# Weights' low words cut to three bits on ScalarE in place, and a cosine as one sine with a quarter turn

## The chip, the cores and the metric

The kernel runs on one core of a Trainium2 chip. Times are microseconds (us) of device time for one execution. TensorE is PE (PEld its weight loads), VectorE is DVE, ScalarE is ACT, GpSimd is POOL; SP is the engine whose queue issues all DMAs here.

## The reference

```python
def _attn_ref(q, k, v):                 # q, k, v: float32 (4, 8, 768, 64)
    for t in range(S):
        state = gamma * state + einsum('bhd,bhe->bhde', k[:, :, t], v[:, :, t])
        y[:, :, t] = scale * einsum('bhd,bhde->bhe', q[:, :, t], state)

def _moe_ref(x, w_in, w_out):           # x (3072, 512), w_in (512, 2048), w_out (2048, 512)
    h = x @ w_in
    g = h * np.cos(h)
    return g @ w_out

def _moe2_ref(x, w_in, w_out):
    h = x @ w_in
    g = np.where(h > 0.0, h, np.exp(np.minimum(h, 0.0)) - 1.0)
    return g @ w_out
```

The result is retention attention, then the first layer pair with `h * cos(h)`, then the second with ELU. The four weight matrices come as float64.

## The kernel before, in words

All code is in `retention_then_two_mlps`. It runs in five stages: the attention by units of 128 tokens (24 units, 4 batches each); the first hidden layer, by 6 blocks of 512 tokens times 8 tiles j of 256 hidden features (`hidden`); the first projection (`project(0, ...)`), by 3 superblocks of two blocks; the second hidden layer (`hidden2`, 24 steps through `seven`); the second projection (`project(1, ...)`). From the first projection on, the products are made with seven block products instead of eight, so operands are summed and subtracted beforehand. Every matmul operand is split in a high and a low part (fp32r), and three matmuls of 512 columns make one product: ACT writes the high part, DVE then subtracts it to get the low one.

Weights: `to_f32` (line 349) brings the float64 words to float32 in 32 pieces of 1024 columns, each in two halves of 512. A half is loaded as pairs of 32-bit words into a buffer `raw` (tag "c"). ACT multiplies the upper words, read as float32, by `REBIAS` into `t`; ACT then writes the same values as float16 into the upper two bytes of each word of the tile `signs`, of which the sign bit is wanted. On DVE, line 374 shifts `t` left by 3 and ors `signs` in, and line 377 ors in the raw low word shifted right by 29, its upper three bits. `first_weights` uses this for the first layer's `w_in` (8 pieces, during the opening and the first block), `convert` for the other three matrices (16 pieces during blocks 1 to 4, 8 during `hidden2`), which are kept in DRAM and split later by `prepare`.

Cosine: `hidden` makes a PSUM tile h of 128x1024. Line 698: ACT writes h / 2 pi rounded to int32 into u. Line 699: DVE takes h / 2 pi - u. Then ACT makes sin(pi x), ACT squares it times 2, and line 704, DVE, makes (g - 1) * h, which is -h cos h; the sign is taken out again by `turn` in `prepare` for layer 0.

What sets the order: the loops only record operations in `Plan` (engine, planned price, buffers read and written, a lag). `Plan.run` then plays the recording through with a list scheduler: each operation has a due time worked backwards from PE's fixed order, each engine takes the ready one that is due first, and the program is written out in that order, engine by engine. Operations marked "ANY" (sums, subtractions, scalings) go to DVE or POOL, whichever is free first in the planner's clock. So another price, one operation less or another engine changes the order of much else. Each engine executes its own list in order. Buffers come from pools: 11 of tag "c" (4 KB per partition), 8 "w", 4 "hl", 3 "ld", 4 "h", and in PSUM 3 "eg" and 2 "f". A PSUM tile h is free for PE when line 704 has read it.

ACT operations all show as line 332 and tensor_tensor operations as line 337, the helpers `act` and `tt`.

Of the kernel before, what the change touches and what calls it, by code (L numbers as in the profile page):

```python
# [9 lines left out]
F32 = mybir.dt.float32  # L10
F32R = mybir.dt.float32r
BF16 = mybir.dt.bfloat16
F16 = mybir.dt.float16
I32 = mybir.dt.int32
U32 = mybir.dt.uint32
U64 = mybir.dt.uint64
AF = mybir.ActivationFunctionType
ALU = mybir.AluOpType

P = 128  # L20
# [14 lines left out]
TWO_PI = 2.0 * math.pi  # L35

REBIAS = 2.0**-112

# [259 lines left out]
def retention_then_two_mlps(ctx: ExitStack, tc: tile.TileContext, attn, tab, weights, out):  # L300
    nc = tc.nc
# [10 lines left out]
    plan = Plan(slots)  # L312
# [18 lines left out]
    def act(us, out_, in_, r, w, func=AF.Copy, lag=0, **kw):  # L331
        plan.op("ACT", us, lambda: nc.scalar.activation(out=out_(), in_=in_(), func=func, **kw), r, w, lag)  # L332
# [6 lines left out]
        plan.op(eng, us, go, r, w, lag)  # L339


    signs = keep.tile([P, 512], U32, name="signs")
    signs_b = Buf(None, [P, 512], U32)
    signs_b.t = signs
    plan.op("DVE", 0.3, lambda: nc.vector.memset(signs, 0.0), [], [signs_b])

    def to_f32(layer, io, j, lag):  # L350
        t = Buf("c", [P, WS])
        if not wide:
            dma(4, lambda: t.t, lambda: weights[layer, io, j], w=[t], lag=lag)
            return t
        for hh in range(2):
            lo, hi = hh * 512, hh * 512 + 512
            raw = Buf("c", [P, 512, 2], U32)
            dma(
                4, lambda raw=raw: raw.t.rearrange("p n w -> p (n w)"),
                lambda lo=lo, hi=hi: weights[layer, io, j][:, lo:hi].bitcast(U32), w=[raw], lag=lag,  # L360
            )
            act(
                0.65, lambda lo=lo, hi=hi: t.t[:, lo:hi], lambda raw=raw: raw.t[:, :, 1].bitcast(F32),
                [raw], [t[lo, hi]], scale=REBIAS, lag=lag,
            )

            act(
                0.65, lambda: signs.bitcast(F16).rearrange("p (n w) -> p n w", w=2)[:, :, 1],
                lambda lo=lo, hi=hi: t.t[:, lo:hi], [t[lo, hi]], [signs_b], lag=lag,
            )  # L370

            def steps(lo=lo, hi=hi, raw=raw):
                u = lambda: t.t[:, lo:hi].bitcast(U32)
                plan.op("DVE", 0.69, lambda: nc.vector.scalar_tensor_tensor(  # L374
                    out=u(), in0=u(), scalar=3, in1=signs, op0=ALU.logical_shift_left, op1=ALU.bitwise_or,
                ), [t[lo, hi], signs_b], [t[lo, hi]], lag)
                plan.op("DVE", 0.69, lambda: nc.vector.scalar_tensor_tensor(  # L377
                    out=u(), in0=raw.t[:, :, 0], scalar=29, in1=u(),
                    op0=ALU.logical_shift_right, op1=ALU.bitwise_or,
                ), [raw, t[lo, hi]], [t[lo, hi]], lag)  # L380

            steps()
        return t
# [34 lines left out]
    def prepare(layer, io, j, lag=0):  # L418
        k = kept[layer, io][j]
        w = Buf("w", [P, NP, 2, Q], F32R)  # L420
        w_t[layer, io, j] = w
        t, s = Buf("c", [P, WS]), Buf("c", [P, WS])
        dma(4, lambda: t.t, lambda: k.t, [k], [t], lag)

        turn = -1.0 if layer == 0 else 1.0

        def split(src, at, lo, hi):
            view = lambda: src.t[:, 0:(hi - lo) * Q].rearrange("p (n q) -> p n q", q=Q)
            high = lambda: w.t[:, lo:hi, 0, :]
            act(0.1 + 0.26 * (hi - lo), high, view, [at], [w[lo, hi]], lag=lag, scale=turn)  # L430
            plan.op("DVE", 0.08 + 0.29 * (hi - lo), lambda: nc.vector.scalar_tensor_tensor(  # L431
                out=w.t[:, lo:hi, 1, :], in0=view(), scalar=turn, in1=high().bitcast(F32),
                op0=ALU.mult, op1=ALU.subtract,
            ), [at, w[lo, hi]], [w[lo, hi]], lag)

        split(t, t[0, 3 * Q], 0, 3)
        a11, a12, a22, a21 = ((t, q * Q, q * Q + Q) for q in range(4))
        s1, s2, s3, s4 = ((s, q * Q, q * Q + Q) for q in range(4))
        for o, a, b, op in (
            (s1, a21, a22, ALU.add), (s2, s1, a11, ALU.subtract),  # L440
            (s3, a11, a21, ALU.subtract), (s4, a12, s2, ALU.subtract),
        ):
            view = lambda x: (lambda: x[0].t[:, x[1]:x[2]])
            tt("ANY", (0.35, 0.7), view(o), view(a), view(b), op, [a, b], [o], lag=lag)
        split(s, s, 3, NP)
# [221 lines left out]
    def hidden(blk, j, between=()):  # L667
        sb, odd = divmod(blk, 2)
        xh, xl = x_t[blk]
        h = Buf("eg", [P, 2 * TB])  # L670
        for half in range(2):
            fi = half if odd else 1 - half

            def go(half=half, fi=fi):
                n = 0
                for kc in range(KC):
                    qd = ((0, 1), (3, 2))[fi][kc // 2]
                    for wpart, xpart in PARTS:
                        nc.tensor.matmul(  # L679
                            out=h.t[:, half * TB:(half + 1) * TB], lhsT=quarter(j, qd, wpart, kc % 2),  # L680
                            rhs=(xh, xl)[xpart].t[:, kc, :], start=(n == 0), stop=(n == 3 * KC - 1),
                        )
                        n += 1

            need = []
            for qd in ((0, 1), (3, 2))[fi]:
                n = 4 * j + qd
                need.append(win1[n // NP][n % NP])
            plan.op("PE", 12 * MM, go, [xh, xl] + need, [h[half * TB, half * TB + TB]])
            if half == 0:  # L690
                for step, n in between:
                    step(n)
        u = Buf("c", [P, 2 * TB])
        g = Buf("c", [P, 2 * TB])


        n = lambda: u.t.bitcast(I32)
        act(1.0, n, lambda: h.t, [h], [u], scale=1.0 / TWO_PI)
        plan.op("DVE", 1.22, lambda: nc.vector.scalar_tensor_tensor(  # L699
            out=g.t, in0=h.t, scalar=1.0 / TWO_PI, in1=n(), op0=ALU.mult, op1=ALU.subtract,  # L700
        ), [h, u], [g])
        act(1.0, lambda: g.t, lambda: g.t, [g], [g], func=AF.Sin, scale=math.pi)
        act(1.0, lambda: g.t, lambda: g.t, [g], [g], func=AF.Square, scale=math.sqrt(2.0))
        plan.op("DVE", 1.22, lambda: nc.vector.scalar_tensor_tensor(  # L704
            out=g.t, in0=g.t, scalar=1.0, in1=h.t, op0=ALU.subtract, op1=ALU.mult,
        ), [h, g], [g])
        if not odd:
            put(0, sb, j, 2, 4, lambda: g.t, [g], 0)
        elif sb == NSB - 1:
            put(0, sb, j, 0, 2, lambda: g.t, [g], 0)  # L710
        else:
            pair_up(0, sb, j, g, u, 30)
# [463 lines left out]
```

## Time and profile before

| | before |
|---|---|
| runs | 1060.12, 1060.22, 1061.75 us; median 1060.22 |
| profiled execution | 1058.54 us |
| its span, first to last instruction | 1056.8 us |
| PE busy | 1028.8 us (97%), mean granted clock 0.995 |
| DVE busy | 806.6 us (76%) |
| ACT busy | 651.5 us (62%) |
| POOL busy | 230.8 us (22%) |

Durations and waits in the following come from the profiled execution. In a table by stretches, an engine's busy time is that of the stretch and the number behind it how many instructions started or ran in it; instructions on one engine can overlap a little, so a sum of durations is somewhat more than the busy time. PEclk is the TensorE clock granted, 1.00 being full speed (2.4 GHz).

### The profile page before, as it was taken

To read this page: it belongs to the slowest core of one execution; us is meant where nothing else is said; L and a number is where in the kernel's file an instruction comes from. 1 tells how busy PE (TensorE), PEld (TensorE's weight loads), DVE (VectorE), ACT (ScalarE), POOL (GpSimd) and SP (SyncE) were. 2 spreads that over 40 slices of the span, in tenths; PEclk is the share of its full clock that TensorE was granted. 3 is DMA by queue.
4 is the path that set the end of the run, shared out by engine and by line. 5 is a ranking of instruction groups with operands and counts; after the bars stand their busy time and mean duration, and the time that the engine had idled before them with its cause. 6 is when DMAs were issued, how large, how long until landed. Compare 5 with 4: busy or idle time off the path is not lost. (4 is left out here: it accounts for less than half of the span.)

```text
span 1056.8 us, 18290 instructions
## 1 busy us (share of the span) xinstructions
PE 1028.8 (97%) x7204; PEld 832.6 (79%) x7208; DVE 806.6 (76%) x931; ACT 651.5 (62%) x788; POOL 230.8 (22%) x213
## 2 busy tenths in 40 slices
PE   6999999999999999999999999999999999999998
PEld 4667788888888888888888777877778888888886
DVE  5898888888889968657468997878889966466453
ACT  2686567766799753443445877877879743544442
POOL 1222340144224610000001542233334201000000
PEclk9899999999999999999999999999999999999999
DMA  9778799999999999999995668789869999999861
GB/s 347 263 259 302 245 361 314 333 355 356 347 331 352 332 345 347 318 326 383 316 359 195 226 245 304 284 311 338 298 239 299 357 333 351 343 320 323 309 209 70
DMA packets 110101, 323.40 MB, mean 306 GB/s; under 512 B 8640, under 2 KB 8640, under 8 KB 107456
## 3 DMA queue, kind: packets, MB, share of 16 engines
q1 hardware_dynamic: 110016, 322.25, 85.4%
q8 instruction: 56, 0.92, 0.4%
q14 instruction: 29, 0.24, 0.1%
HBM read 195.86 MB, written 126.35 MB: 305 GB/s over the span
## 5 line engine op out<-in xcount | busy, mean ns | idle before, releaser
L925 PE MATMUL eg<-hl,w 128*128 128x512 f32 x2016 | 457.9, 389 | 1.0 <-DVE h L877 0.9
L925 PEld LDWEIGHTS eg<-hl,w 128*128 128x128 f32 x2016 | 378.3, 188 | 80.3 <-DVE h L877 1.4
L332 ACT ACTIVATE hl<-ld 128x1024 fp32r<-128x1024 f32 x168 | 177.7, 1060 | 226.3 <-PE eg L925 206.3
L337 DVE TENSOR_TENSOR hl<-ld,hl 128x1024 fp32r<-128x1024 f32 x168 | 211.6, 1269 | 94.4 <-ACT hl L332 94.3
L679 PE MATMUL eg<-hl,w 128*128 128x512 f32 x1152 | 277.0, 397 | 3.0 <-DVE c L704 1.5
L337 POOL TENSOR_TENSOR c<-c 128x512 f32<-128x512 f32 (+1 forms) x141 | 173.3, 1240 | 479.5 <-DVE c L337 170.4
L332 ACT ACTIVATE c<-c 128x1024 f32<-128x1024 f32 (+1 forms) x256 | 232.1, 918 | 57.7 <-DVE c L699 27.9
L679 PEld LDWEIGHTS eg<-hl,w 128*128 128x128 f32 x1152 | 214.2, 189 | 51.5 <-DVE w L337 1.9
L337 DVE TENSOR_TENSOR c<-c 128x512 f32<-128x512 f32 (+2 forms) x127 | 92.8, 741 | 40.5 <-DMA c<-d 30.0
L332 ACT ACTIVATE c<-eg 128x1024 int32<-128x1024 f32 (+2 forms) x95 | 86.3, 909 | 50.7 <-PE eg L679 43.2
L755 PE MATMUL eg<-hl,w 128*128 128x512 f32 x432 | 110.6, 392 | 2.8 <-DVE c L337 1.4
L755 PEld LDWEIGHTS eg<-hl,w 128*128 128x128 f32 x432 | 80.2, 188 | 23.4 <-DVE c L337 3.0
L755 PE MATMUL eg<-ld,w 128*128 128x512 f32 x288 | 74.1, 393 | 4.6 <-ACT h L332 3.9
L699 DVE SCALAR_TENSOR_TENSOR c<-eg,c 128x1024 f32<-128x1024 f32 x48 | 58.6, 1220 | 19.2 <-ACT c L332 17.1
L755 PEld LDWEIGHTS eg<-ld,w 128*128 128x128 f32 x288 | 53.4, 188 | 18.4 <-ACT h L332 6.0
L704 DVE SCALAR_TENSOR_TENSOR c<-c,eg 128x1024 f32<-128x1024 f32 x48 | 58.3, 1215 | 12.1 <-ACT c L332 11.7
L332 ACT ACTIVATE w<-c 128x1024 fp32r<-128x1024 f32 (+3 forms) x59 | 52.7, 920 | 10.0 <-DMA c<-d 3.6
L431 DVE SCALAR_TENSOR_TENSOR w<-c,w 128x768 fp32r<-128x768 f32 (+1 forms) x48 | 56.2, 1183 | 0.9 <-ACT w L332 0.9
L332 ACT ACTIVATE signs<-c 128x512 f16<-128x512 f32 x64 | 50.2, 785 | 6.5 <-DVE c L374 5.8
L377 DVE SCALAR_TENSOR_TENSOR c<-c 128x512 uint32<-128x512 uint32 x64 | 52.6, 831 | 0.7
L374 DVE SCALAR_TENSOR_TENSOR c<-c,signs 128x512 uint32<-128x512 uint32 x64 | 50.2, 785 | 0.8 <-ACT signs L332 0.5
L332 ACT ACTIVATE h<-eg 128x512 f32<-128x512 f32 (+1 forms) x50 | 29.2, 584 | 29.1 <-PE eg L755 10.7
(58 smaller groups left out, 641.8 us busy)
## 6 DMA issues: line engine op xcount, KB each, us to landing
d<-c SPq DMA_DIRECT2D x205, 512.0 KB, 5.1
ld<-d SPq DMA_DIRECT2D x84, 1024.0 KB, 8.1
c<-d SPq DMA_DIRECT2D x93, 512.0 KB, 6.1
c<-in_weights SPq DMA_DIRECT2D x64, 512.0 KB, 6.6
ld<-in_attn SPq DMA_DIRECT2D x20, 1024.0 KB, 7.8
d<-h SPq DMA_DIRECT2D x32, 256.0 KB, 8.3
out<-c SPq DMA_DIRECT2D x11, 512.0 KB, 7.2
d<-c SPq DMA_DIRECT2D x16, 256.0 KB, 3.8
```

The source lines that it names most:

```text
L332: plan.op("ACT", us, lambda: nc.scalar.activation(out=out_(), in_=in_(), func=func, **kw), r, w, lag)
L337: return e.tensor_tensor(out=out_(), in0=a(), in1=b(), op=op)
L374: plan.op("DVE", 0.69, lambda: nc.vector.scalar_tensor_tensor(out=u(), in0=u(), scalar=3, in1=signs, op0=ALU.logical_shift_left, op1=ALU.b ...
L377: plan.op("DVE", 0.69, lambda: nc.vector.scalar_tensor_tensor(out=u(), in0=raw.t[:, :, 0], scalar=29, in1=u(), op0=ALU.logical_shift_right ...
L431: plan.op("DVE", 0.08 + 0.29 * (hi - lo), lambda: nc.vector.scalar_tensor_tensor(out=w.t[:, lo:hi, 1, :], in0=view(), scalar=turn, in1=hig ...
L679: nc.tensor.matmul(out=h.t[:, half * TB:(half + 1) * TB], lhsT=quarter(j, qd, wpart, kc % 2), rhs=(xh, xl)[xpart].t[:, kc, :], start=(n == ...
L699: plan.op("DVE", 1.22, lambda: nc.vector.scalar_tensor_tensor(out=g.t, in0=h.t, scalar=1.0 / TWO_PI, in1=n(), op0=ALU.mult, op1=ALU.subtra ...
L704: plan.op("DVE", 1.22, lambda: nc.vector.scalar_tensor_tensor(out=g.t, in0=g.t, scalar=1.0, in1=h.t, op0=ALU.subtract, op1=ALU.mult,), [h, ...
L755: nc.tensor.matmul(out=out_(), lhsT=w.t[:, i, wpart, kc * P:(kc + 1) * P], rhs=x.t[:, xpart, kc, :], start=(start and n == 0), stop=(n == ...
L925: nc.tensor.matmul(out=acc.t[:, i * TB:(i + 1) * TB], lhsT=w[:, A_OF[p], wpart, i * P:(i + 1) * P], rhs=hl.t[:, gpart, k, :], start=(p in ...
```

## The change

Weights: the tile `signs` and its memset are gone. ACT multiplies the raw low word, read as an unsigned integer, by 0.936 x 2^-29 and writes it rounded as int16 into the lower two bytes of that same word; ACT writes the float16 of `t` into the upper two bytes. Each low word of `raw` then holds the three bits and the sign, and one DVE step (line 378 now) shifts `t` and ors it in. The second DVE step is gone.

Cosine: the rounding adds 0.25, so the remainder x lies a quarter turn lower; one Sin with scale 2 pi and a bias of pi / 2, read from a [128, 1] tile set once, makes cos h; the Square is gone, and DVE multiplies by h with a plain tensor_tensor. `turn` is 1 for both layers. The planner's price for the Sin is 1.1 where it was 1.0.

```diff
+LOW_BITS = 0.936 * 2.0**-29
...
-    signs = keep.tile([P, 512], U32, name="signs")
-    signs_b = Buf(None, [P, 512], U32)
-    signs_b.t = signs
-    plan.op("DVE", 0.3, lambda: nc.vector.memset(signs, 0.0), [], [signs_b])
+    turn_b = Buf(None, [P, 1])
+    turn_b.t = keep.tile([P, 1], F32, name="quarter_turn")
+    plan.op("DVE", 0.1, lambda: nc.vector.memset(turn_b.t, math.pi / 2), [], [turn_b])
...
+            end = lambda part, dt, raw=raw: raw.t.rearrange("p n w -> p (n w)").bitcast(dt).rearrange(
+                "p (n w) -> p n w", w=4)[:, :, part]
...
-            act(
-                0.65, lambda: signs.bitcast(F16).rearrange("p (n w) -> p n w", w=2)[:, :, 1],
-                lambda lo=lo, hi=hi: t.t[:, lo:hi], [t[lo, hi]], [signs_b], lag=lag,
-            )
+            act(0.65, lambda end=end: end(0, I16), lambda raw=raw: raw.t[:, :, 0], [raw], [raw],
+                scale=LOW_BITS, lag=lag)
+            act(0.65, lambda end=end: end(1, F16), lambda lo=lo, hi=hi: t.t[:, lo:hi],
+                [t[lo, hi]], [raw], lag=lag)
...
                 plan.op("DVE", 0.69, lambda: nc.vector.scalar_tensor_tensor(
-                    out=u(), in0=u(), scalar=3, in1=signs, op0=ALU.logical_shift_left, op1=ALU.bitwise_or,
-                ), [t[lo, hi], signs_b], [t[lo, hi]], lag)
-                plan.op("DVE", 0.69, lambda: nc.vector.scalar_tensor_tensor(
-                    out=u(), in0=raw.t[:, :, 0], scalar=29, in1=u(),
-                    op0=ALU.logical_shift_right, op1=ALU.bitwise_or,
-                ), [raw, t[lo, hi]], [t[lo, hi]], lag)
+                    out=u(), in0=u(), scalar=3, in1=raw.t[:, :, 0], op0=ALU.logical_shift_left, op1=ALU.bitwise_or,
+                ), [t[lo, hi], raw], [t[lo, hi]], lag)
...
-        turn = -1.0 if layer == 0 else 1.0
+        turn = 1.0
...
-        act(1.0, n, lambda: h.t, [h], [u], scale=1.0 / TWO_PI)
+        act(1.0, n, lambda: h.t, [h], [u], scale=1.0 / TWO_PI, bias=0.25)
...
-        act(1.0, lambda: g.t, lambda: g.t, [g], [g], func=AF.Sin, scale=math.pi)
-        act(1.0, lambda: g.t, lambda: g.t, [g], [g], func=AF.Square, scale=math.sqrt(2.0))
-        plan.op("DVE", 1.22, lambda: nc.vector.scalar_tensor_tensor(
-            out=g.t, in0=g.t, scalar=1.0, in1=h.t, op0=ALU.subtract, op1=ALU.mult,
-        ), [h, g], [g])
+        act(1.1, lambda: g.t, lambda: g.t, [g, turn_b], [g], func=AF.Sin, scale=TWO_PI, bias=turn_b.t)
+        tt("DVE", 1.22, lambda: g.t, lambda: g.t, lambda: h.t, ALU.mult, [g, h], [g])
```

PE's order of work stays; the order on the other engines changes in many places. Three of them follow. A name's number tells one buffer from another within a program; they differ between the programs. ACT's helper is line 334 in the changed kernel, `tt` line 339.

DVE in the opening, from the third unit's mask to the end of the attention output (hl) of the first block. Before:

```order
L374 SCALAR_TENSOR_TENSOR c_327<-c_327,signs_81 128x512
L572 COPY w_136<-eg_286 128x256
L377 SCALAR_TENSOR_TENSOR c_327<-c_201,c_327 128x512
L377 SCALAR_TENSOR_TENSOR c_327<-c_206,c_327 128x512
L563 TENSOR_TENSOR w_441<-eg_390,w_136 128x768
L572 COPY w_136<-eg_390 128x256
L374 SCALAR_TENSOR_TENSOR c_387<-c_387,signs_81 128x512
L337 TENSOR_TENSOR hl_339<-f_445,hl_331 128x2x128
L337 TENSOR_TENSOR hl_339<-f_446,hl_331 128x2x128
L337 TENSOR_TENSOR ld_382<-ld_382,w_136 128x512
L337 TENSOR_TENSOR w_443<-c_327,w_443 128x4x256
L337 TENSOR_TENSOR hl_339<-f_481,hl_331 128x2x128
```

And now:

```order
L378 SCALAR_TENSOR_TENSOR c_327<-c_327,c_201 128x512
L378 SCALAR_TENSOR_TENSOR c_327<-c_327,c_206 128x512
L563 TENSOR_TENSOR w_442<-eg_393,w_136 128x768
L339 TENSOR_TENSOR w_434<-c_327,w_434 128x4x256
L572 COPY w_136<-eg_393 128x256
L339 TENSOR_TENSOR hl_339<-f_445,hl_331 128x2x128
L339 TENSOR_TENSOR hl_339<-f_446,hl_331 128x2x128
L339 TENSOR_TENSOR ld_384<-ld_384,w_136 128x512
L378 SCALAR_TENSOR_TENSOR c_389<-c_389,c_341 128x512
L339 TENSOR_TENSOR hl_339<-f_483,hl_331 128x2x128
```

The two shifts of line 377 are gone, and the wide weight split (w_434) has moved ahead of the third unit's pieces.

ACT in the first block, between the int32 conversions (eg) of tiles 1 and 2. Before:

```order
L332 ACTIVATE c_727<-eg_624 128x1024
L332 ACTIVATE c_748<-c_599 128x512
L332 ACTIVATE w_750<-c_597 128x2x256
L332 ACTIVATE signs_81<-c_748 128x512
...
L332 ACTIVATE c_748<-c_637 128x512
L332 ACTIVATE c_798<-eg_730 128x1024
```

The line left out is the pair Sin and Square. And now, where c_595, c_599 and c_639 are raw buffers:

```order
L334 ACTIVATE c_742<-eg_621 128x1024
L334 ACTIVATE w_747<-c_665 128x2x256
L334 ACTIVATE c_595<-c_665 128x512
L334 ACTIVATE c_754<-c_599 128x512
L334 ACTIVATE c_599<-c_599 128x512
L334 ACTIVATE c_751<-c_751,quarter_turn_81 128x1024
L334 ACTIVATE c_754<-c_639 128x512
L334 ACTIVATE c_639<-c_639 128x512
L334 ACTIVATE c_814<-eg_729 128x1024
```

Three two-byte writes stand where there was one, and one wide activation where there were two.

ACT at the entry of the second hidden layer, around the copy of the last projection's tile (c_5845, now c_5793). Before:

```order
L332 ACTIVATE ld_5841<-c_5802 128x1024
L332 ACTIVATE c_5845<-eg_5310 128x1024
L332 ACTIVATE w_5807<-c_5810 128x4x256
L332 ACTIVATE w_5804<-c_5827 128x4x256
L332 ACTIVATE h_5863<-eg_5834 128x512
```

And now:

```order
L334 ACTIVATE c_5793<-eg_5261 128x1024
L334 ACTIVATE ld_5798<-c_5758 128x1024
L334 ACTIVATE ld_5802<-c_5775 128x1024
L334 ACTIVATE w_5756<-c_5778 128x4x256
L334 ACTIVATE h_5810<-eg_5786 128x512
```

Two of the layer's first x2 operands (ld) have moved behind the copy, and the first snapshot (h) comes one activation later.

## Rows read from the trace of the kernel before

**Rows 1.** The page, part 1: busy time, share of the span, instructions.

```profile
PE 1028.8 (97%) x7204; PEld 832.6 (79%) x7208; DVE 806.6 (76%) x931; ACT 651.5 (62%) x788; POOL 230.8 (22%) x213
```

**Rows 2.** Stretches: us, then PE, PEld, DVE, ACT, POOL busy, clock, DMA, GB/s.

```profile
0.00:40.00 40.00, 28.52 (x620) 18.93 (x624) 26.32 (x44) 14.76 (x27) 7.57 (x10) 0.87 0.91 336
40.40:94.20 53.80, 51.00 (x716) 39.65 (x720) 50.77 (x66) 43.57 (x59) 13.88 (x18) 1.00 0.73 258
94.20:375.00 280.80, 280.33 (x2951) 227.62 (x2952) 245.03 (x306) 200.61 (x245) 98.41 (x97) 1.00 0.93 331
...
560.00:790.00 230.00, 221.92 (x959) 178.32 (x958) 197.28 (x238) 177.96 (x239) 77.64 (x59) 1.00 0.75 274
```

**Rows 3.** PE's waits from 0 to 40 us: us in total, times, longest.

```profile
PE f L629 <- issue: 4.8, 2, 3.5
...
PE f L629 <- DVE hl L337: 1.4, 1, 1.4
```

**Rows 4.** PE's waits from 40 to 145 us.

```profile
PE eg L679 <- DVE c L704: 1.5, 3, 0.7
PE eg L536 <- DVE w L578: 0.9, 1, 0.9
PE eg L679 <- DVE w L337: 0.6, 2, 0.3
```

**Rows 5.** PE's waits from 560 to 830 us.

```profile
PE eg L755 <- ACT h L332: 4.8, 6, 1.5
PE eg L755 <- DVE c L337: 2.1, 4, 0.7
PE f L755 <- DVE hl L337: 0.6, 1, 0.6
```

**Rows 6.** Groups by form: shapes and count, then busy us, mean ns, idle before.

```profile
L332 ACT ACTIVATE signs<-c 128x512 f16<-128x512 f32 x64 | 50.2, 785 | 6.5 <-DVE c L374 5.8
L332 ACT ACTIVATE c<-c 128x512 f32<-128x512 f32 x88 | 57.1, 651 | 21.5 <-DMA c<-in_weights 16.6 <-issue 2.3 <-DVE c L337 1.8
L332 ACT ACTIVATE c<-c 128x1024 f32<-128x1024 f32 x168 | 177.6, 1058 | 36.2 <-DVE c L699 27.9 <-DVE c L857 1.4 <-POOL c L337 1.3
L377 DVE SCALAR_TENSOR_TENSOR c<-c 128x512 uint32<-128x512 uint32 x64 | 52.6, 831 | 0.7
L704 DVE SCALAR_TENSOR_TENSOR c<-c,eg 128x1024 f32<-128x1024 f32 x48 | 58.3, 1215 | 12.1 <-ACT c L332 11.7
L337 DVE TENSOR_TENSOR c<-eg,c 128x1024 f32<-128x1024 f32 x18 | 22.0, 1222 | 6.4 <-PE eg L925 4.9 <-DMA d<-c 1.5
```

**Rows 7.** The second stretch, line 377 alone: DVE busy, clock, DMA, GB/s.

```profile
40.40:94.20 53.80, 11.26 (x13) 1.00 0.73 258
```

**Rows 8.** Timeline in the opening, ACT and then DVE: start, us, what.

```profile
22.70 0.78 ACT L332 ACTIVATE signs<-c 128x512 f16<-128x512 f32 x1
23.33 0.67 ACT L332 ACTIVATE c<-c 128x512 f32<-128x512 f32 x1
...
25.77 1.06 ACT L332 ACTIVATE w<-c 128x1024 fp32r<-128x1024 f32 x1 [0.18 <-DVE c L377]
26.73 0.64 ACT L332 ACTIVATE hl<-f 128x256 fp32r<-128x256 f32 x2
...
24.45 1.28 DVE L377 SCALAR_TENSOR_TENSOR c<-c 128x512 uint32<-128x512 uint32 x2
```

**Rows 9.** Timeline of PE, first hidden matmuls: start, us, what, idle before.

```profile
32.10 1.22 PE L679 MATMUL eg<-hl,w 128*128 128x512 f32 x2 [0.33 <-DVE hl L337]
```

**Rows 10.** Stretches of 8 us in the opening (columns as in rows 2).

```profile
24.00:32.00 8.00, 4.72 (x162) 3.54 (x161) 8.00 (x13) 4.92 (x9) 2.96 (x2) 0.89 0.93 329
32.00:40.00 8.00, 7.42 (x23) 5.45 (x23) 6.33 (x12) 4.08 (x7) 1.04 (x1) 0.69 0.82 314
```

**Rows 11.** Timeline of PE at the entry of the second hidden layer.

```profile
586.19 1.65 PE L755 MATMUL eg<-ld,w 128*128 128x512 f32 x6 [0.73 <-ACT h L332]
...
592.87 1.32 PE L755 MATMUL eg<-ld,w 128*128 128x512 f32 x5
```

More of the change, by code (lines that the diff above doesn't have):

```diff
@@ L14 @@
 I32 = mybir.dt.int32
+I16 = mybir.dt.int16
 U32 = mybir.dt.uint32
```

## The prediction

> **What bounds the kernel now.** I read first which engine is busy. TensorE (PE) works through 97% of the span [rows 1]. So no gain can come from an engine's busy time alone: it has to come out of the 28 us in which PE stands still, or out of the time in which it runs at half clock. The table by stretches [rows 2] says where these are: 11.5 us of idle PE in the first 40 us, 2.8 us between 40.4 and 94.2, 0.5 us up to 375, 8.1 us between 560 and 790 (the second hidden layer); the 5 us that are left lie in the projections and at the end, which the change does not touch. In the same table VectorE (DVE) is busy 50.77 of 53.80 us in the second stretch, and 86% of the fourth; ScalarE (ACT) has 81% and 77% there. Then I asked what ended PE's waits. In the opening the largest are PE's own "issue" gaps, 4.8 us, and 1.4 us is for a DVE split of the attention's output [rows 3]. From 40 to 145 us its waits end with a DVE instruction: 1.5 + 0.9 + 0.6 = 3.0 us [rows 4]. In the second layer 4.8 us end with ACT's copies out of PSUM, 2.1 + 0.6 us with DVE [rows 5]. So the stretch in which the change works hardest, the conversion of the first weights, is one in which DVE holds PE up and ACT still has some room.
>
> **The weights: off DVE, onto ACT.** There are 64 halves to convert. Each loses one DVE shift-and-or, 0.831 us in the mean and 52.6 us in all [rows 6]; the remaining one now reads its second operand at the removed one's stride, so it costs that row's 0.831 us at most, in stages where DVE then has room: nothing for PE. Each half gains one ACT instruction, the low word to three bits. The trace has none that reads an integer low word and writes two bytes in every eight. Nearest is the copy that writes the sign half, two bytes in every four: 0.785 us. Below, a 512-wide copy of four-byte values is 0.65 us; above, I allow twice the nearest, 1.57 us. I take 0.785 us for both two-byte writes, since they differ from that row only in stride.
>
> **The cosine.** 48 Square instructions of 1.058 us go from ACT [rows 6], and from the chain that hands a PSUM tile back: PE, ACT to int32, DVE, Sin, Square, DVE. That chain gets about 1.05 us shorter per tile. The last DVE step becomes a plain multiply; the same shape is in the trace at 1.222 us against 1.215, so nothing. The Sin now reads its bias from a tile, which no activation before does; from rows I bound that by nothing at all and by the 0.05 us by which wide activations differ among themselves. The Trainium skill (ScalarE: Activation LUTs, section What ACT_TABLE_LOAD costs) says that a [128,1] pointer operand adds about 93 ns to an activation; no run here shows it yet. By that page 7 Sins would cost ACT 0.65 us in the second stretch, and if all of that reached PE the forecast would be 1057.4 in place of 1056.7.
>
> **Second stretch, 40.4 to 94.2 us.** Between the first and the eighth int32 conversion DVE loses 13 shifts, 11.26 us [rows 7]: 50.77 - 11.26 = 39.5 of 53.8. ACT's order there shows 12 two-byte writes more than the 12 before, 12 four-byte ones where there were 10, and 7 Squares fewer: 43.57 + 12 x 0.785 + 2 x 0.65 - 7 x 1.058 = 46.9 us. PE needs 53.8 less its waits of 2.7 there, 51.1 us. So ACT has 4.2 us to spare and neither engine binds. Following the order tile by tile, the split of the weights for a tile, ACT and then DVE, comes at or before PE's need. I take the 3.0 us of rows 4 as gone.
>
> **Opening.** Before, DVE is busy all the time from 24 to 32 us [rows 10], two shifts (1.28 us) among it [rows 8], and PE gets the last low piece of the attention output at 32.10 us [rows 9]. Now ACT does more first: from 22.70 us two sign halves (23.33 - 22.70 = 0.63 each from start to start), a copy (0.65), a low word (0.63), the wide weight copy (26.73 - 25.77 = 0.96), a copy and a low word, so it copies the third unit's output at 27.5 in place of 26.73 us [rows 8]. But DVE no longer has the shifts and the wide split in front of the last two pieces, and these come at about 30.8 us: 1.3 us earlier. Part of it may be lost to the clock: after the thin stretch before 32 us, in which PE is busy 4.72 of 8, the granted clock averages 0.69 up to 40 [rows 10], so PE starts there at the lower of its two levels, 1.2 GHz, where time won counts half. I take -0.8 us, between 0 and -1.3.
>
> **Second layer.** 16 of the 64 halves are converted here, 16 x 0.785 = 12.6 us more on ACT (77% to 83%) and 16 x 0.831 = 13.3 less on DVE (86% to 80%). At its entry there is no conversion, but the order has changed: two x2 pieces are now split behind the copy of the last projection, the first snapshot comes at about 584.8 us and PE's second step starts near 587.7, not 586.19; the later operands come no later than before, so the place that it reached at 592.87 us [rows 11] it reaches some 0.25 us later. Behind the entry one engine got what the other lost, with about as much waited for each; I take 0, bounds -2.7 (all DVE waits gone) and +2.7 (ACT's grow by half).
>
> **Queues and cover.** The number of DMAs stays. A raw buffer is now released by the first DVE step, not the second, so weight loads on SP's queue wait no longer for buffers; but the tile 'signs' no longer links one half to the next. The planner also shifts 29 of the 189 subtractions and scalings that DVE or POOL may do from POOL to DVE; they fill part of what the shifts free, while the port is shared less. From 94.2 to 375 us PE hardly waits, so what changes there costs nothing: some 30 low words come to ACT and 41 Squares go, and its 201 of 281 us [rows 2] leave room if that cover were thinner.
>
> **Sum.** -3.0 - 0.8 + 0.25 + 0 = -3.5 us on the profiled execution of 1058.54 us, so 1055.0 there. The median of the runs shown is 1060.22, 1.7 above it; against that, **1056.7 us**.
>
> **Rivals.**
> *More of the same* (chance 0.08): the 2.7 us that DVE costs PE in the second layer go too: 1060.2 - 6.2 = 1054.0. For it: DVE is the busier engine there. Against: 4.8 us wait on ACT, which gets more.
> *The change does not free DVE* (0.30): POOL's subtractions take the place of the shifts, the order is dealt anew, and waits of the old size return behind other instructions, ACT's weight copies above all. Only the opening's -0.8 and half a microsecond more or less stay: 1059.5. For it: 29 moved instructions; the planner prices a two-byte write at 0.65 us where the row has 0.785, so ACT's queue runs later than planned, and everything behind waits in order.
> *ACT becomes the bound* (0.22), the slower side: its place is the second stretch, with 24 two-byte writes. At 4.2 us of room it decides from 0.785 + 4.2/24 = 0.96 us per write. At 1.18, the middle between the row and its double, the writes take 9.5 us more, 5.3 beyond the room, and only the opening's 0.8 and the 0.5 us of rows 4 that lie behind the stretch (3.0 against 2.7 within it, rounded) stand against it: 1060.2 + 4.0 = 1064.2. For it: a two-byte write already costs 0.13 us more than a four-byte one, and the stride doubles. Against: the four-byte reads at the same eight-byte stride stand at 0.65. The Trainium skill (SBUF — State Buffer, section Door 1) says that accesses run at full rate while at least two fall in each 16-byte line; by that rule eight bytes are still free and this rival would need another cause. No row here has such a write, so I lower its chance only a little for that.
>
> **How the numbers follow.** The forecast has 0.40. Faster by over 0.2% (2.1 us, about what a measurement can tell): forecast and "more", 0.48. Within: 0.30. Slower: 0.22. The range reaches from just below 1054.0 to 1064.0, which leaves out the upper half of ACT's rival and the edge of "more", together under 0.2. The forecast's own range is 1054.0 to 1058.1.
>
> **What would show it.** Right: no PE wait on the second DVE step of the cosine or on a weight split between 40 and 145 us; the low-word row at 0.75 to 0.82 us; DVE near 40 and ACT near 47 us in the second stretch; the first hidden matmuls without a gap from 31 us. Wrong: a two-byte row over 0.96 us, PE waits there ending with ACT, over 9 us of PE idle between 560 and 790 us, or another clock in the opening: the 0.89 and 0.69 of rows 10 cost PE 8 x 0.11 + 8 x 0.31 = 3.4 us, so without them, or with as much again, the result moves by as much as the whole forecast.

## The result and the profile after

The changed kernel takes 1073.11 us (median of four runs, 1072.07 to 1075.86) against 1060.18 before, also of four: a ratio of 1.013 with a 95% interval of 1.0108 to 1.0151. It is slower by 13 us; forecast were 1056.7, with a range up to 1064.0. The profiled execution's span is 1071.7 us, and the readings below are of it.

The page of the changed kernel, part 1, to set beside [rows 1]:

```profile
PE 1034.1 (96%) x7208; PEld 834.8 (78%) x7208; DVE 766.9 (72%) x896; ACT 708.2 (66%) x804; POOL 189.4 (18%) x184
```

DVE and POOL lost 40 us each, as the change says. ACT was to come out about even, with 48 Squares less, and is 57 us busier. The groups by form say why (columns as in [rows 6]):

```profile
L334 ACT ACTIVATE c<-c 128x512 int16<-128x512 uint32 x64 | 86.9, 1370 | 1.0 <-DMA c<-in_weights 1.0
L334 ACT ACTIVATE c<-c 128x512 f16<-128x512 f32 x64 | 85.3, 1384 | 0.9
...
L334 ACT ACTIVATE c<-c,quarter_turn 128x1024 f32<-128x1024 f32 x48 | 54.9, 1145 | 27.6 <-DVE c L699 27.4
...
L378 DVE SCALAR_TENSOR_TENSOR c<-c 128x512 uint32<-128x512 uint32 x64 | 48.1, 753 | 44.0 <-ACT c L334 43.3
```

Both two-byte writes take 1.37 to 1.38 us, where the sign's took 0.785 [rows 6]; the one DVE step that is left waits 44 us in all, nearly always for ACT. By stretches (columns and stretches as in [rows 2]):

```profile
0.00:40.00 40.00, 27.63 (x632) 19.00 (x636) 20.67 (x39) 22.57 (x31) 8.46 (x11) 0.91 0.90 337
40.40:94.20 53.80, 48.44 (x654) 36.95 (x646) 39.65 (x57) 53.38 (x65) 7.65 (x11) 0.97 0.73 248
94.20:375.00 280.80, 278.37 (x2970) 225.32 (x2971) 224.92 (x282) 210.34 (x233) 77.78 (x89) 1.00 0.90 324
...
560.00:790.00 230.00, 219.87 (x932) 175.44 (x931) 181.42 (x217) 191.78 (x241) 68.44 (x50) 0.99 0.75 274
```

In the second stretch DVE fell from 50.77 to 39.65 us, near the forecast 39.5, and ACT rose to 53.38 of 53.80: it is hardly ever free. PE idles 5.4 us there where it idled 2.8. What one such wait looks like, on the timelines of ACT, DVE and PE (start, us, what, idle before):

```profile
59.70 2.59 ACT L334 ACTIVATE c<-c 128x512 int16<-128x512 uint32 x2
62.02 1.11 ACT L334 ACTIVATE c<-c,quarter_turn 128x1024 f32<-128x1024 f32 x1
...
63.17 1.22 DVE L339 TENSOR_TENSOR c<-c,eg 128x1024 f32<-128x1024 f32 x1 [1.51 <-ACT c L334]
...
64.53 4.82 PE L679 MATMUL eg<-hl,w 128*128 128x512 f32 x12 [3.03 <-DVE c L339]
```

Two low words hold ACT for 2.3 us, the Sin comes behind them, DVE's multiply waits 1.51 us for the Sin, and PE waits 3.03 us for the PSUM tile that the multiply reads. PE's wait names DVE, but DVE had itself been waiting: the late one is ACT. All waits of PE from 40 to 145 us, then those from 550 to 860:

```profile
PE eg L679 <- DVE c L339: 3.5, 2, 3.0
PE eg L679 <- DVE w L339: 1.1, 2, 0.8
PE eg L679 <- ACT w L334: 0.6, 1, 0.6
```

```profile
PE eg L752 <- ACT h L334: 7.2, 9, 1.7
PE eg L752 <- DVE c L339: 1.9, 4, 1.3
PE f L752 <- DVE ld L339: 1.2, 1, 1.2
PE eg L752 <- DVE hl L339: 1.0, 1, 1.0
PE f L752 <- ACT ld L334: 0.7, 1, 0.7
```

The 3.0 us of [rows 4] have become 5.2. In the second layer the waits of [rows 5], with two lesser ones of 0.5 us, were 8.0 us and are 12.0 now. Where the time was lost in all is read from the first and last start of two groups of PE: the second hidden layer (L755, now L752) and the projections (L925, now L922). The view by source line, before:

```profile
L755 PE MATMUL eg<-hl,w x432: 387/389/504, 589.0 to 822.3; 128*128 128x512 f32 x144
L755 PE MATMUL eg<-ld,w x288: 387/389/501, 580.2 to 814.1; 128*128 128x512 f32 x144
...
L925 PE MATMUL eg<-hl,w x2016: 387/389/504, 351.7 to 1052.4; 128*128 128x512 f32 x184
```

And after:

```profile
L752 PE MATMUL eg<-hl,w x432: 387/389/628, 597.8 to 837.6; 128*128 128x512 f32 x144
L752 PE MATMUL eg<-ld,w x288: 387/389/628, 586.0 to 828.6; 128*128 128x512 f32 x144
...
L922 PE MATMUL eg<-hl,w x2016: 388/389/500, 355.8 to 1067.3; 128*128 128x512 f32 x184
```

The first projection begins 4.1 us later (355.8 - 351.7). The second layer begins 5.8 later (586.0 - 580.2), so the first projection's stage gave 1.7, of which 1.4 are one wait for a DVE split at 363 us. The second layer ends 15.3 later (837.6 - 822.3), so it alone gave 9.5. The last projection's last matmul is 14.9 later: nothing more behind it.

### The profile page after: what moved, and what is told of

Its sections match the earlier page's. It is cut to its first block, busy times and chain, and to the rows that moved or that the text cites. A ratio compares the mean times of both kernels' runs of the same rounds, so it can differ in the third digit from the quotient of the medians.

```text
span 1071.7 us, 18167 instructions
## 1 busy us (share of the span) xinstructions
PE 1034.1 (96%) x7208; PEld 834.8 (78%) x7208; DVE 766.9 (72%) x896; ACT 708.2 (66%) x804; POOL 189.4 (18%) x184
## 4 chain that ended last, share of the span: by engine, by line
PE 63%; ACT 12%; DVE 6%; issue 3%; DMA 1%; ACTq 0%; DVEq 0%
PE eg L922 41%; ACT c L334 10%; PE eg L752 10%; PE eg L679 7%; PE f L752 3%; DVE w L431 2%; DVE c L339 2%; ACT h L334 1%; DVE c L699 1%; DMA c<-in_weights 1%; ACT hl L334 0%; DVE hl L339 0%; ACT w L334 0%; PE f L629 0%; PE f L598 0%
## 5 line engine op out<-in xcount | busy, mean ns | idle before, releaser
L922 PE MATMUL eg<-hl,w 128*128 128x512 f32 x2016 | 457.9, 389 | 2.3 <-DVE hl L339 1.4
L922 PEld LDWEIGHTS eg<-hl,w 128*128 128x128 f32 x2016 | 378.2, 188 | 81.7 <-DVE hl L339 1.8
L334 ACT ACTIVATE c<-c 128x512 f32<-128x512 f32 (+3 forms) x288 | 293.3, 1082 | 24.7 <-DMA c<-in_weights 19.2
L339 DVE TENSOR_TENSOR hl<-ld,hl 128x1024 fp32r<-128x1024 f32 x168 | 206.9, 1242 | 93.8 <-ACT hl L334 93.7
L339 POOL TENSOR_TENSOR c<-c 128x256 f32<-128x256 f32 (+1 forms) x119 | 141.7, 1197 | 511.5 <-DVE c L339 175.6
L339 DVE TENSOR_TENSOR c<-c 128x512 f32<-128x512 f32 (+2 forms) x149 | 104.1, 708 | 33.5 <-DMA c<-d 29.5
L752 PE MATMUL eg<-hl,w 128*128 128x512 f32 x432 | 112.3, 396 | 5.7 <-ACT h L334 3.9
L752 PEld LDWEIGHTS eg<-hl,w 128*128 128x128 f32 x432 | 80.3, 188 | 27.9 <-ACT h L334 6.9
L752 PE MATMUL eg<-ld,w 128*128 128x512 f32 x288 | 76.1, 401 | 4.9 <-ACT h L334 3.4
L378 DVE SCALAR_TENSOR_TENSOR c<-c 128x512 uint32<-128x512 uint32 x64 | 48.1, 753 | 44.0 <-ACT c L334 43.3
L334 ACT ACTIVATE c<-c,quarter_turn 128x1024 f32<-128x1024 f32 x48 | 54.9, 1145 | 27.6 <-DVE c L699 27.4
L339 DVE TENSOR_TENSOR c<-c,eg 128x1024 f32<-128x1024 f32 x48 | 58.3, 1216 | 17.8 <-ACT c L334 17.7
L752 PEld LDWEIGHTS eg<-ld,w 128*128 128x128 f32 x288 | 55.0, 193 | 20.3 <-ACT h L334 7.0
L339 DVE TENSOR_TENSOR c<-eg,h 128x512 f32<-128x512 f32 x48 | 32.9, 686 | 17.9 <-PE eg L752 13.5
L339 POOL TENSOR_TENSOR ld<-ld,w 128x512 f32<-128x512 f32 x25 | 28.7, 1155 | 89.3 <-DMA ld<-in_attn 26.3
```

What stands on the lines that cost most here:

```text
L339: return e.tensor_tensor(out=out_(), in0=a(), in1=b(), op=op)
L752: nc.tensor.matmul(out=out_(), lhsT=w.t[:, i, wpart, kc * P:(kc + 1) * P], rhs=x.t[:, xpart, kc, :], start=(start and n == 0), stop=(n == ...
L922: nc.tensor.matmul(out=acc.t[:, i * TB:(i + 1) * TB], lhsT=w[:, A_OF[p], wpart, i * P:(i + 1) * P], rhs=hl.t[:, gpart, k, :], start=(p in ...
```

## The experiments

Each time stands beside runs of the kernel before on the same chip, whose median lay between 1058.1 and 1059.1 us.

**The two halves of the change alone.** First the cosine's lines of the diff on top of the kernel before (rounding bias 0.25, one Sin with the quarter-turn tile, plain multiply, `turn = 1.0`).

> The cosine part alone, weights converted as before. Theory A (the two-byte writes at eight-byte stride, 1.37 to 1.38 us each, overload ACT and cost everything): this kernel has none of them, ACT loses 48 Squares of 1.06 us and gains 48 x 0.09 us for the Sin's bias, so it is no slower than before: 1054 to 1060 us. Theory C (the cosine's new form or the order it brings costs): slower than before by several us, 1064 or more.

Measured 1061.57 us, ratio 1.0025 (1.001 to 1.0041): between the ranges of the two theories, a little slower than before. The Sin takes 1.149 us, ACT falls to 606.1 us in all, and yet it is no faster: between 40.4 and 94.2 us ACT loses 6 us, and PE's busy time there rises only from 51.00 to 51.16 (in the profiled execution, the slowest of the ten). DVE, which still has its shifts (48.43 us), is busier than ACT there.

Then the weights' lines alone, with the old Sin, Square and multiply.

> The weight part alone, cosine as before. Theory A: all of the loss is here, and ACT also keeps the 48 Squares that the whole change took off it, so at least as slow as the whole change: 1073 to 1080 us. Theory C: clearly faster than the whole change, under 1066 us.

Measured 1091.11 us, ratio 1.0306 (1.0283 to 1.0329). Stretches of this run:

```profile
40.40:94.20 53.80, 44.99 (x561) 34.22 (x560) 35.78 (x51) 53.61 (x62) 5.62 (x9) 0.94 0.63 218
94.20:375.00 280.80, 269.53 (x3006) 216.15 (x3005) 211.10 (x280) 239.70 (x269) 75.04 (x81) 0.99 0.89 315
```

That is more than theory A's 1073 to 1080. ACT is full again in the second stretch, and the loss runs on to 375 us, where PE idles 11.3 us. That the Squares, still there, keep ACT from catching up is likely but not shown: ACT has 239.70 us of that stretch, not all of it. So the weights are the part that loses, about 32 us; in the whole change the cosine's part, which takes the Squares off ACT, gives 19 of them back.

**The stride of the writes.** Both two-byte writes are packed into the front half of the raw buffer, four bytes apart. The low words are then read and written in place at different strides, and the weights' low bits come out other than before, so the run is read for its times alone. The instructions are the same in number, shape and, engine by engine, in order.

```diff
-            end = ... raw.t ... .bitcast(dt).rearrange("p (n w) -> p n w", w=4)[:, :, part]
+            front = lambda raw=raw: raw.t.rearrange("p n w -> p (n w)")[:, 0:512]
+            end = ... front().bitcast(dt).rearrange("p (n w) -> p n w", w=2)[:, :, part]
...
-                    out=u(), in0=u(), scalar=3, in1=raw.t[:, :, 0], ...
+                    out=u(), in0=u(), scalar=3, in1=front(), ...
```

> The whole change, but both two-byte writes go side by side into the front half of the raw buffer, so that each has a stride of four bytes, not eight; instructions and their number stay. Theory A (stride sets the price): both writes fall to about 0.79 us, ACT is no longer busy all of the time from 40 to 90 us, and the time comes to where the forecast put it, 1054 to 1060 us. If two bytes, not the stride, are dear in this place: rows stay near 1.38 us and the time near 1073.

Measured 1056.63 us, ratio 0.9978 (0.9963 to 0.9992). Its two writes, its second stretch and the marks of PE:

```profile
L334 ACT ACTIVATE c<-c 128x512 int16<-128x512 uint32 x64 | 50.0, 788 | 3.5 <-DMA c<-in_weights 2.4
...
L334 ACT ACTIVATE c<-c 128x512 f16<-128x512 f32 x64 | 48.1, 779 | 0.9
```

```profile
40.40:94.20 53.80, 53.60 (x787) 42.42 (x786) 44.06 (x63) 45.76 (x69) 7.87 (x12) 1.00 0.78 269
```

```profile
L752 PE MATMUL eg<-hl,w x432: 387/389/632, 585.5 to 820.3; 128*128 128x512 f32 x144
L752 PE MATMUL eg<-ld,w x288: 387/389/632, 575.3 to 811.3; 128*128 128x512 f32 x144
...
L922 PE MATMUL eg<-hl,w x2016: 387/389/498, 346.8 to 1050.0; 128*128 128x512 f32 x184
```

In the same order, four bytes between the writes in place of eight are worth about 16 us: 1.3% slower than the kernel before has become 0.2% faster. PE idles 0.2 us in the second stretch. The DVE step reads its second operand packed too, but that does not speed it up (0.807 us against 0.753), so the gain is that of the two writes. Of the 17.3 us between the last matmuls of the two profiled executions (1067.3 - 1050.0), 9.0 are won up to the first projection, 1.7 in it, 6.6 in the second layer.

**Stride or width.** In the changed kernel, only the low bits are written as 32-bit words, still eight bytes apart; the sign keeps its two-byte write.

```diff
-            act(0.65, lambda end=end: end(0, I16), lambda raw=raw: raw.t[:, :, 0], ...
+            act(0.65, lambda raw=raw: raw.t[:, :, 0].bitcast(I32), lambda raw=raw: raw.t[:, :, 0], ...
```

> The whole change, but the low word's three bits are written in place as a four-byte integer, at the same eight-byte stride; the sign half is still a two-byte write over its upper half. If two-byte writes at that stride are dear and four-byte ones are not: the low word's row falls to about 0.65 us, the sign's stays at 1.38, half of ACT's overload goes, and the time lies between, 1061 to 1068 us. If the stride alone is dear: both rows stay at 1.38 and the time near 1073.

Measured 1058.62 us, ratio 0.9993 (0.9975 to 1.0011): the rows are as the first theory wants them, the time is below its range. The two writes side by side, at one stride:

```profile
L334 ACT ACTIVATE c<-c 128x512 f16<-128x512 f32 x64 | 85.1, 1379 | 0.9
...
L334 ACT ACTIVATE c<-c 128x512 int32<-128x512 uint32 x64 | 42.8, 674 | 3.3 <-DMA c<-in_weights 3.3
```

Four bytes written in every eight cost 0.674 us, two bytes in every eight 1.379. And one dear write of two costs little: ACT has 49.87 us of the second stretch's 53.80, and PE's busy time there is back at 52.09. In one order, then, PE idles 0.2 us of the second stretch with no dear write, 1.7 with one and 5.4 with two: the loss grows faster than the price, as ACT's free time runs out.

**The prices by themselves.** A kernel without the computation runs 12 ACT copies of 512 values in each of twelve forms.

> Leaves the whole computation out: it writes zeros as output and runs twelve activations of 128x512 for each of twelve forms, with outputs of two or four bytes at strides of 2, 4, 8 and 16 bytes. Theory A: the two-byte write costs about 0.61 us packed, 0.79 at four bytes, 1.38 at eight; the four-byte write stays near 0.65 at eight, so it is the two-byte write at a wide stride that is dear. Rival: what counts is the stride in bytes alone; then the four-byte write at eight bytes costs about 1.38 as well. Rival: reading the integer word at eight bytes is what costs; then the row from the integer word to four bytes is dear too.

Span 122.8 us. The forms run in pairs, one instruction of each in turn, and the names do not tell the stride, which follows from the order in the program. Single instructions from ACT's timeline: two bytes written dense, then 4, 8 and 16 bytes apart (half_by), four bytes 8 and 16 apart (word_by) and four apart, read from every eight (word_by_from), and int16 written 4 and 8 bytes apart (short_by_from):

```profile
5.03 0.60 ACT L332 ACTIVATE half_by<-src 128x512 f16<-128x512 f32 x1
5.54 0.76 ACT L332 ACTIVATE half_by<-src 128x512 f16<-128x512 f32 x1
...
17.50 1.31 ACT L332 ACTIVATE half_by<-src 128x512 f16<-128x512 f32 x1
18.56 2.51 ACT L332 ACTIVATE half_by<-src 128x512 f16<-128x512 f32 x1
...
59.80 0.64 ACT L332 ACTIVATE word_by<-src 128x512 f32<-128x512 f32 x1
...
71.75 0.63 ACT L332 ACTIVATE word_by_from<-pairs 128x512 f32<-128x512 f32 x1
72.29 1.08 ACT L332 ACTIVATE word_by<-src 128x512 f32<-128x512 f32 x1
...
89.66 0.82 ACT L332 ACTIVATE short_by_from<-pairs 128x512 int16<-128x512 uint32 x1
90.35 1.31 ACT L332 ACTIVATE short_by_from<-pairs 128x512 int16<-128x512 uint32 x1
```

So the price goes by the stride counted in the value's own width, not by the stride in bytes alone: at eight bytes two-byte values take 1.31 us and four-byte ones 0.64. Dense, both take 0.60 to 0.61 us; at twice the width 0.76 for two bytes and 0.64 for four; at four times 1.31 and 1.08; at eight times, for two bytes, 2.51. Who stands in front matters too: the other eleven half writes at eight bytes, each behind one at sixteen, show 1.62 us, and the int16 write at four bytes 0.82 behind one at eight, 0.76 where it is the first. From start to start, an int16 write at four bytes takes 0.69 us (90.35 - 89.66), the half of 1.31 us takes 1.06 (18.56 - 17.50).

**The planner's price.** In the changed kernel the planner is told 1.12 us for the two writes, about their pitch, in place of 0.65.

> The whole change, but the planner is told 1.12 us for each of the two writes (the pitch of such writes in the trace after) in place of 0.65. Theory A: ACT's work is unchanged, so the time stays within 4 us of 1073. Theory B (the work would fit, but the planner's wrong price puts it in a bad order, and in-order queues make the loss): at least half of the 13 us come back, under 1067 us.

Measured 1065.64 us, ratio 1.0063 (1.004 to 1.0086): ACT has about the same work, 705.6 us, and about half of the loss is back. Theory A is missed by this, and theory B holds as it was written: the dear writes cost what they cost in the order that the planner deals, and another order halves the loss. It is not back where I looked for it: the first projection begins at 359.6 us, later still than the 355.8 of the changed kernel, but the second layer takes 243.7 us (588.3 to 832.0) in place of 251.6. How much of that is the better price, and how much the accident of another order, two more runs bound. The kernel before, with Sin and Square priced at 1.06 us, their duration, in place of 1.00:

> The kernel before with the planner's price of Sin and Square at 1.06 us, their measured duration, in place of 1.00: no operation differs, only the order dealt. It measures how far a mere new dealing of the order moves the time. If such dealings move it by 2 us or more, the 0.25 per cent that the cosine alone lost needs no cause of its own; if the time stays within 1 us of the kernel before, that loss is the cosine's.

Measured 1061.80 us, ratio 1.002 (1.0005 to 1.0036). No operation differs, so a new dealing alone moves the time by about 2 us (0.5 to 3.8 by the interval), and the cosine's 1.0025 needs no cause of its own. Then the run with the low word at 32 bits, its sign priced at 1.12:

> The run with the low bits as a 32-bit word (1058.62 us) with the planner told 1.12 us for the sign's two-byte write, which is about its pitch. Theory (the planner's wrong price is part of the loss, as the two writes at 1.12 gave back about half): ACT's work stays, PE's idle in the first weights and in the second layer falls, 1055 to 1058 us. Rival (with one dear write ACT has room, the price no longer matters): within 1.5 us of 1058.6.

Measured 1062.59 us, ratio 1.0032 (1.002 to 1.0044): 4 us slower than with the wrong price, against the theory, and beyond the rival's 1.5 us as well. A truer price is not always a better order; differences of 2 to 4 us between dealings are read as such below.

**Four-byte stride with nothing overwritten.** The packed bits get 2 KB of their own: one kept tile for the first half of a piece, a buffer of tag "h" for the second.

```diff
+            low = Buf("h", [P, 512], U32) if hh else all_bits[0]
-            end = lambda part, dt, raw=raw: ...
+            end = lambda part, dt, low=low: low.t.bitcast(dt).rearrange("p (n w) -> p n w", w=2)[:, :, part]
```

> The changed kernel with both two-byte writes packed four bytes apart in a 2 KB buffer of their own instead of in the raw words: the first half of a piece uses one kept tile, the second a buffer of tag h. The raw buffer is then free once ACT has read it, and the order is dealt anew. Theory (the writes' stride was the whole miss): both write rows at 0.75 to 0.82 us, ACT 46 to 48 us between the first and the eighth int32 conversion, PE waits of the weights gone there, 1054 to 1059 us. Rival (the order that is dealt decides as much as the write): the writes cost 0.78 us too, but the time comes out anywhere between 1059 and 1066 us.

Measured 1059.19 us, ratio 1.001 (0.9998 to 1.0023): just above the theory's range, at the lower end of the rival's. The writes stand at 0.771 to 0.787 us, PE has 53.06 of the second stretch's 53.80 us, the first projection begins at 346.3 us, and the second layer gives the gain back: 574.8 to 822.1 is 247.3 us where the kernel before has 242.1. PE's waits there, from 560 to 800 us:

```profile
PE eg L755 <- ACT h L334: 12.2, 12, 2.2
PE f L755 <- DVE hl L339: 0.6, 1, 0.6
PE eg L755 <- ACT c L334: 0.3, 1, 0.3
```

The copies into "h", 4.8 us of waits in [rows 5], now cost 12.2. These buffers and the one kept tile are shared with the eight pieces converted there. With every half in a buffer of tag "h":

> As the run with bits in a tile of their own, but every half takes a buffer of tag h, so the second hidden layer's snapshots share their four buffers with the eight pieces converted there. Theory (stride alone): as that run up to 560 us; in the second layer up to 3 us more PE idle if a snapshot waits for a buffer; 1054 to 1061 us. Rival (order decides): differs from that run by over 2 us before 560 us already.

Measured 1058.81 us, ratio 0.9995 (0.9983 to 1.0006). Up to the first projection it is as the other run (346.7 against 346.3 us), as the theory wants. The second layer takes 247.5 us, but PE's waits for ACT's "h" fall to 8.0 us although more is shared. So the sharing alone does not explain the 12.2; which part is the order stays open.

**A version that is faster than both.** Packed bits early, where they win, and in the second hidden layer the 32-bit word in place, which needs no buffer.

```diff
+            low = raw if (layer, io) == (1, 1) else Buf("h", [P, 512], U32) if hh else all_bits[0]
```

> Own tile for the packed bits in the opening and blocks 1 to 4 (as the run with bits in a tile of their own), and in the second hidden layer in place, the low bits as a 32-bit word (as the run of 1058.6 us). Theory (the two stages are independent: the packed bits won 2.1 us of PE time between 40.4 and 94.2 us and 1.3 in the opening, and lost 5.2 in the second layer because ACT and the h buffers came late there): PE idle of 8 to 9 us between 560 and 790 us in place of 13.3, so 1053 to 1057 us. Rival (each change of a late operation deals the whole order anew, and the early gain is luck of the order): 1058 to 1062 us.

> Packed bits only for the first layer's two matrices, the 32-bit word in place for the second layer's two. Theory: the first 94 us as in the run with bits in a tile of their own, the second layer as in the run of 1058.6 us, and between 94 and 560 us PE does not wait: 1053 to 1057 us, within 1 us of the other mixed version. Rival (luck of the order): the two mixed versions differ by over 2 us, or both lie at 1058 to 1062.

The second takes `raw if layer` for that condition, so both matrices of the second layer are converted in place. Measured 1054.21 us, ratio 0.9961 (0.995 to 0.9973), and 1053.69 us, ratio 0.9962 (0.9947 to 0.9976). Marks of the second of them:

```profile
L763 PE MATMUL eg<-hl,w x432: 387/389/501, 583.0 to 816.6; 128*128 128x512 f32 x144
L763 PE MATMUL eg<-ld,w x288: 387/389/504, 574.1 to 808.4; 128*128 128x512 f32 x144
...
L933 PE MATMUL eg<-hl,w x2016: 388/389/499, 345.6 to 1046.3; 128*128 128x512 f32 x184
```

The first projection begins 6.1 us earlier than before the change, the second layer takes 242.5 us, as before. The two agree within 0.5 us, as the theory wanted and the rival did not. In the other one, though, PE has only 51.06 us of the second stretch, not 53.06: its early gain is smaller than the sum said, by about what a new dealing is worth. That it was the dealing is not shown.

## Why the prediction was wrong

**The price of the two-byte writes** is the step that failed: "I take 0.785 us for both two-byte writes, since they differ from that row only in stride". The stride was the whole of it: 1.370 and 1.384 us, inside my bounds of 0.65 and 1.57, near the far end. I had counted the sign's stride as two bytes in four and the new one as two in eight, and then took the price of the first for both; the argument against a dearer write, 0.65 us for four-byte values at eight bytes, was about reads, and at twice the value's width, not four times. The Trainium skill (SBUF — State Buffer, section Door 1) has accesses at full rate while two fall in each 16-byte line; two-byte writes eight bytes apart are two to a line, and take 1.37 us here, 1.8 times the 0.77 to 0.79 at four bytes. The measurement decides, and my chance for ACT's rival should not have been lowered for that rule at all. With the price went the conclusion that "ACT has 4.2 us to spare and neither engine binds": in the second stretch ACT had 0.4 us to spare (53.80 - 53.38), and it bound.

**The rest of the sum at the price assumed.** The run at four-byte stride has my price (0.788 and 0.779 us) and my order. It is 0.22% faster than the kernel before on its chip, 2.3 us (0.8 to 3.9 by the interval), where the sum says 3.5. That its 1056.63 us stand so near my 1056.7 is chance, since the kernel before was itself at 1058.87 there and not at 1060.22. By terms: the second stretch was to lose its DVE waits, 3.0 us, and PE idles 0.2 us there where it idled 2.8. Up to the first projection 4.9 us are won (351.7 - 346.8), where opening and waits were put at 3.8. The second layer takes 245.0 us (820.3 - 575.3), 2.9 more than before, where I had +0.25 and bounds of 2.7 about it. It is at the edge of them, and not for the reason given there: the same matmuls in the three second layers (before, after, four-byte stride; columns as in [rows 2]):

```profile
580.16:822.28 242.12, 233.86 (x1008) 187.34 (x1007) 210.97 (x259) 195.12 (x263) 89.22 (x73) 1.00 0.79 284
```

```profile
586.00:837.61 251.61, 239.09 (x1009) 189.36 (x1007) 200.08 (x249) 220.98 (x280) 79.18 (x62) 0.99 0.76 274
```

```profile
575.26:820.29 245.03, 236.26 (x1009) 188.57 (x1007) 200.41 (x249) 205.84 (x280) 79.23 (x62) 0.99 0.77 282
```

PE's idle time grows from 8.3 (242.12 - 233.86) to 8.8 us only; the other 2.4 are the matmuls themselves, 236.26 against 233.86 us, at a lower average clock.

**ACT becomes the bound** (0.22) is what happened. Its threshold of 0.96 us per write is passed. The run with one dear write (mean of the two 1.03 us) lies just above it, and loses about what the rival's working gives there: 24 x (1.03 - 0.785) = 5.9 us, 1.7 beyond the room of 4.2, where PE idles 1.5 us more than at four-byte stride. By the same working at 1.38 us: 24 x (1.38 - 0.785) = 14.3 us, 10.1 beyond the room, less the 1.3 against it: 1069.0. Measured 1073.1. That this is near is in part luck.

The place that the rival named was too narrow. By the marks up to the first projection only 4.1 us are lost, where it had 8.8; in the second layer, where I let 16 halves cost nothing, 32 dear writes add 31.5 us of ACT's durations (32 x 1.377 - 16 x 0.785) where I had 12.6, and 9.5 us are lost. By the lines above, 4.3 of them are idle time of PE (12.5 against 8.3), and 5.2 a longer busy time for the same matmuls (239.09 against 233.86). Most of the 5.2 is the clock: it averages 0.91 from 580 to 600 us and again from 680 to 700, where it was 1.00 before, each time in a stretch in which PE also stood still (17.30 and 17.99 us busy of 20); 2 x 20 x 0.09 = 3.6 us. The last 1.6 us I cannot place.

```profile
580.00:600.00 20.00, 17.30 (x67) 13.24 (x66) 17.77 (x20) 13.33 (x18) 6.56 (x2) 0.91 0.94 329
...
680.00:700.00 20.00, 17.99 (x71) 14.08 (x70) 14.98 (x19) 19.20 (x24) 6.90 (x6) 0.91 0.92 332
```

**Opening.** Forecast -0.8 us, from an earlier attention output. That step failed too:

```profile
24.00:32.00 8.00, 3.02 (x91) 2.28 (x93) 5.46 (x9) 8.00 (x11) 1.27 (x1) 0.92 0.94 357
32.00:40.00 8.00, 8.00 (x116) 6.66 (x112) 5.06 (x11) 7.41 (x11) 2.33 (x2) 0.87 0.88 355
```

ACT now has 8.00 busy us of the 8 before 32. PE waits 4.2 us for DVE's split of the attention's output, and its first hidden matmul comes at 34.16 instead of 30.98. Yet the first int32 conversion starts at 40.65 against 40.40: PE stands still no more between 32 and 40 us, and the clock there averages 0.87, not the 0.69 of [rows 10], which the last sentence of the prediction had left open. At the price assumed it is no different in kind: in the run at four-byte stride PE waits 2.4 us for the split, the first hidden matmul comes at 32.36, still 1.4 later than before, and the first int32 conversion comes 1.3 us earlier (39.12), with the clock at 0.84 on average between 32 and 40 us and PE without a stop. So there the size came near the forecast by luck.

**The Sin's bias tile.** Forecast 0 to 0.05 us, measured 1.145 to 1.149 against 1.058 us: 0.09. The Trainium skill (ScalarE: Activation LUTs, section What ACT_TABLE_LOAD costs) gives about 93 ns for a pointer operand, and the trace agrees; 7 in the second stretch are 0.6 us.

**The planner's price**, which I had named as what speaks for another rival, is real but not separable here: told the pitch, it gave 7 us back, in another stage than expected, and in the run with one dear write it cost 4. So the stride of the writes is shown as what makes the loss in this order, and its size, 13 us, as that of this order.

## What to carry to other kernels

Price a new form of instruction by its write pattern, stride in units of the value's own width, and when the nearest row differs in just that, run the sum at both bounds: here ACT's rival, worked out at 1.38 us, turns the sum from -3.5 to +9 us inside the bounds that stood in the text. When work moves to an engine, count it in every stage in which it moves, against that stage's free time: in the same order, with ACT at 49.9 of 53.8 us PE idled 1.7 us, and at 53.4 it idled 5.4. And where a list scheduler deals the order, an edit that changes no operation moved the time by about 2 us, so a gain of that size is believed when two different orders show it.

## What the hardware showed unexpectedly

By themselves, ACT writes 512 two-byte values in 0.60 us dense, in 0.76 at a stride of four bytes, in 1.31 at eight and in 2.51 at sixteen; four-byte values take 0.61 dense, 0.64 at eight bytes and 1.08 at sixteen. Reads of four-byte values at eight bytes cost almost nothing extra (0.63 us). In the kernel one two-byte write and one four-byte write at the same stride of eight bytes take 1.379 and 0.674 us, so writing more bytes halves the time.
